# Fusing the weights of keys and queries in 64 by 128 tiles and in two groups, and a first chunk that goes keys, queries, values

## The chip, the cores and the metric

The kernel runs on one core of a Trainium2 chip. The metric is the device time of one execution in microseconds (us). A core has a tensor engine (PE in the profile, with its weight loads shown apart as PEld), a vector engine (DVE), a scalar engine (ACT), a GpSimd engine (POOL) and a queue that issues transfers (SP). Multiplications write to PSUM, which this kernel divides into eight banks of 128 x 512 float32.

## What is computed

The input x has 2048 tokens of 512 numbers. One branch is linear attention with 32 heads of 16 numbers, the other a dense layer with Mish; a sigmoid gate mixes them.

```python
qkv = x @ wqkv                                   # q, k, v: 32 heads of 16
pq, pk = q @ w_phi, k @ w_phi                    # per head, 16 x 16
phi(p) = concat(softmax(p), softmax(-p))         # over the 16, per head: 32 features
kv, z = phi(pk)^T v, sum over tokens of phi(pk)
a = (phi(pq) kv) / (phi(pq) z + 1e-6) @ wo
b = mish(x @ w1 + b1) @ w2
out = g * a + (1 - g) * b,  g = sigmoid((x * gate_w).sum(-1))
```

As pk = (x wk) w_phi = x (wk w_phi), the kernel multiplies the weights first: the 512 x 512 matrix wk with the block-diagonal matrix of w_phi once ("fusing"), and the same for wq. From then on keys and queries are one projection of x each.

## The kernel before

**Two stages.** Stage A runs over 8 chunks of 256 tokens: projections of keys, values and queries, the features of the keys, and the sums over tokens. Stage B runs over 4 blocks of 512 tokens: the dense branch, the features of the queries, the rest of the attention, and the output. The change is all in the first chunk of stage A and in what comes ahead of it.

**Split numbers.** Each float32 operand of a large multiplication is split into a rounded high part and the rest, its low part (names end in h and l): wkh and wkl, xh and xl. A projection of 128 tokens (`proj`, L228) is 12 multiplications of 128 x 512: four 128-row pieces of the depth (k = 0 to 3), times high by high, low by high and high by low. The high part is a copy on ACT (L117), the low part a subtraction on DVE or POOL.

**Fusing.** `fuse` (L214) works for one depth piece k of one matrix. For each of four groups G of eight heads, it multiplies a 128 x 128 block of the transposed weights (as the stationary operand) with a 64 x 64 block of the block-diagonal matrix. L220 does it in four tiles of 64 x 64: two halves r of the rows, each of which has its own PSUM bank, and two halves c of the stationary columns. These operands are plain float32, and the profile shows each such multiplication as two (a load and a multiplication each): 32 loads for one k.

**The order at the start.** SP issues the transfers in the order of the program: wk's first piece, then pieces of x's first chunk and of wk in turn (L147 to L153), both halves of wv (L160), the four pieces of wq (L161), x's second chunk (L163). PE warms up with ten multiplications of ones (L174). The code from L739 on then sets the order on each engine by hand:

- fuse k = 0 and 1 of the keys into four banks (tag "dn"); `fsplit` (L723) splits them, 256 columns at a time, on ACT and DVE; x's first half is split too (`x_one`, L751).
- ten multiplications of the keys' projection (`k_part`, L742, L773), for both 128-token halves in turn; then fuse k = 2 and 3 (L775), two more multiplications, the split of these pieces, and the split of wv: high part on ACT, low part on DVE (L782, L783). The twelve multiplications for k = 2 and 3 end the keys' projection (L784).
- `run(FIRST, ...)` (L810) issues the rest of chunk 0 word by word: v0 and v1 are the values' projections, q0 and q1 the queries'; ve and qe copy them out of PSUM, st stores the queries; mx, mn, d0, d1, E, S, rS, ml are the features of the keys (maximum, minimum, two differences, exponential, sum, reciprocal, product) and z adds them up on POOL; xh and xl split the next chunk's x; ldx and ldw load a later chunk and pieces of w1. The word fq is the fusing of all four pieces of wq in one burst (L790), fh and fl are their splits. So the order on PE is: keys, v0, fusing of wq, v1, q0, q1.

**PSUM.** A pool gives banks in rotation by tag: "a" has three, "dn" four, "kv" one. A bank is written again when its readers are done. Each later chunk goes keys, values, queries by the text MID, with keys and queries in "a" and values in "dn". The sum over tokens (`kv`) takes the bank "kv" from the third chunk on.

Of the kernel before, what the change touches and what calls it, by code (L numbers as in the profile page):

```python
# [19 lines left out]
KT = D // P  # L20
# [15 lines left out]


FIRST = """
    v0 mx0 mn0 d00 d10 mx1 mn1 d01 d11 fq ve0 E0 fh0 fh1 fl0 fl1 fh2 fh3 fl2 fl3 E1 xh xl ldx v1 ve1
    S0 rS0 ml0 z0 ldw0 ldw1 S1 rS1 ml1 z1 q0 qe0 st0 q1 qe1 st1  # L40
"""
MID = """
    k0 xh mx0 mn0 d00 d10 xl ldx k1 wh0 E0 wl0 ldw0 mx1 mn1 d01 d11 v0 wh1 E1 S0 rS0 ml0 z0 ve0 v1 wl1 ldw1
# [42 lines left out]
def tile_gated_mix(ctx: ExitStack, tc: tile.TileContext, xT, wv, wkT, wqT, bd, w1a, w1b, b1, w2a, w2b, wo, out):  # L86
# [6 lines left out]
    pin = tc.keep_in_program_order  # L93
    V, G_, A_, Sy = nc.vector, nc.gpsimd, nc.scalar, nc.sync

    def mm(*a, **k):
        return pin(nc.tensor.matmul(*a, **k))  # L97
# [14 lines left out]
    def psum(name, tag, bufs={"a": 3, "dn": 4, "kv": 1}):  # L112
        nm[0] += 1
        return pp.tile([P, 512], F32, name=f"{name}_{nm[0]}", tag=tag, bufs=bufs[tag])

    def act(out_, in_, fn=AF.Copy, **k):
        return pin(A_.activation(out_, in_, fn, **k))  # L117
# [7 lines left out]
    def f32(ap):  # L125
        return ap.bitcast(F32)
# [8 lines left out]
    skT, sqT = stage(wkT), stage(wqT)  # L135
    bds = k2("bds", "io")[:, :].rearrange("p (g f) -> p g f", g=NG)
# [3 lines left out]
    def ldx(c):  # L140
        rawx[c] = k4("xraw", "tx")
        pin(Sy.dma_start(kt(rawx[c], SC), xT[c]))

    def ldk(dst, src, k):
        pin(Sy.dma_start(dst[:, k, :, :], src[:, k, :, :]))
# [9 lines left out]
    def piece(dram, o, n=1024, small=False):  # L155
        r = k2("raw", "hl") if small else k4("raw", "oh")
        pin(Sy.dma_start(r[:, :n], dram[:, o : o + n]))
        return r[:, :n]

    wvr = [piece(wv, o) for o in (0, 1024)]  # L160
    for k in range(KT):  # L161
        ldk(sqT, wqT, k)
    ldx(1)  # L163


# [30 lines left out]
    def at(key, name, fn):  # L196
        steps.setdefault((key, name), []).append(fn)
# [10 lines left out]
    xs, Es, vs, psA, Ep = {}, {}, {}, {}, {}  # L208
# [5 lines left out]
    def fuse(acc, staged, k):  # L214

        for G in range(NG):
            o = (k % 2 * NG + G) * 64
            for r in (0, 64):
                for c in (0, 64):
                    mm(acc[r // 64][c : c + 64, o : o + 64], staged[r : r + 64, k, G, c : c + 64], bds[r : r + 64, G, r : r + 64], start=True, stop=True, skip_group_check=True)  # L220

    def fuse_banks():
        return [psum("fuse", "dn") for _ in range(2)]

    def halves(w, ks):
        return [w[:, ks, :].rearrange("p k (g r f) -> p r (k g) f", r=2, f=64)[:, r, :, :] for r in range(2)]

    def proj(x, t, wh, wl, tag, lo_last=False):  # L228
        ps = psum("proj", tag)
        xh, xl = x  # L230
        sl = slice(t * P, (t + 1) * P)
        n = 0
        for a, w in ((xh, wh), (xl, wh), (xh, wl)) if lo_last else ((xh, wh), (xh, wl), (xl, wh)):
            for k in range(KT):
                mm(ps, a[k // 2][:, k % 2, sl], w[:, k, :], start=(n == 0), stop=(n == 3 * KT - 1))
                n += 1
        return ps
# [49 lines left out]
    def a_ops(c):  # L287
        key = ("A", c)
        P_ = psA[c] = {}
        for t in range(2):  # L290
            d = {}
            Es[c, t] = d

            def k_(t=t):
                P_["k", t] = proj(xs[c], t, wkh, wkl, "a")

            def v_(t=t):
                P_["v", t] = proj(xs[c], t, wvh, wvl, "dn" if c else ("kv", "a")[t], lo_last=not c)

            def q_(t=t):  # L300
                P_["q", t] = proj(xs[c], t, wqh, wql, "a")

            def ve(t=t):
                if key in THIRD:
                    if t == 0:
                        Ep[key, "v"] = T([P, NFB * 512], F32, "w2b", 2, "v")
                    vs[c, t] = Ep[key, "v"][:, t * 512 : (t + 1) * 512]
                else:
                    vs[c, t] = k2("v", "io")
                act(vs[c, t], P_["v", t])  # L310

            def qe(t=t):
                P_["qs", t] = k2("qs", "pq")
                act(P_["qs", t], P_["q", t])

            def st(t=t):
                i = 2 * c + t
                pin(Sy.dma_start(pqd[i * P : (i + 1) * P, :], P_["qs", t]))

            at(key, f"k{t}", k_)  # L320
            at(key, f"v{t}", v_)
            at(key, f"q{t}", q_)
            at(key, f"ve{t}", ve)
            at(key, f"qe{t}", qe)
            at(key, f"st{t}", st)
            feat_ops(key, t, lambda t=t: P_["k", t][:, :], d)
            at(key, f"ml{t}", lambda d=d: scale_by(d, V))
            at(key, f"z{t}", lambda d=d: pin(G_.tensor_add(zacc, zacc, d["E"])))  # L328

        def kv():  # L330
            if not kvs:
                kvs.append(psum("kvp", "kv")[:, : NG * 64].rearrange("p (g f) -> p g f", g=NG))
            (kvp,) = kvs
            for t in range(2):
                E, v = Es[c, t]["E"], vs[c, t]
                Ev = E[:, :].rearrange("p (a r b x) -> p b r a x", a=2, r=2, b=8)
                for u in range(8):
                    for r in range(2):
                        o = (u % 2) * 64 + 32 * r
                        mm(kvp[o : o + 32, u // 2, :], v[:, u * 64 + 32 * r : u * 64 + 32 * r + 32], Ev[:, u, r, :, :],  # L340
                           start=(c == 0 and t == 0 and u < 2), stop=(c == NCH - 1 and t == 1), skip_group_check=True)

        at(key, "kv", kv)
        if c + 1 < NCH:
            def xh():
                new_x(c + 1)
                for j in range(2):
                    x_hi(c + 1, j)

            at(key, "xh", xh)  # L350
            for j in range(2):
                at(key, "xl", lambda j=j: x_lo(c + 1, j, G_))
        if c + 2 < NCH:
            at(key, "ldx", lambda: ldx(c + 2))
# [368 lines left out]
    def fsplit(acc, k):  # L723
        wh, wl = halves(wkh, slice(k, k + 1)), halves(wkl, slice(k, k + 1))
        src = [a[:, k % 2 * 256 : k % 2 * 256 + 256].rearrange("p (g f) -> p g f", f=64) for a in acc]
        def hi():
            act(wh[0], src[0])
            if k:
                act(wh[1], src[1])
            else:  # L730
                pin(V.tensor_copy(wh[1], src[1]))

        def lo():
            for r in range(2):
                pin(V.tensor_sub(wl[r], src[r], f32(wh[r])))

        return hi, lo

    new_x(0)  # L739
    pk = {}  # L740

    def k_part(k, n):  # L742

        a, w = ((xs[0][0], wkh), (xs[0][1], wkh), (xs[0][0], wkl))[n]
        for t in range(2):
            sl = slice(t * P, (t + 1) * P)
            if t not in pk:
                pk[t] = psum("proj", "a")
            mm(pk[t], a[k // 2][:, k % 2, sl], w[:, k, :], start=(k == 0 and n == 0), stop=(k == KT - 1 and n == 2))

    def x_one(k):  # L751

# [4 lines left out]
    def fused(ks):  # L757
        acc = [fuse_banks() for _ in ks]
        for a, k in zip(acc, ks):
            fuse(a, skT, k)  # L760
        return acc

    acc = fused((0, 1))
# [6 lines left out]
    l1()  # L770
    x_hi(0, 1)
    x_lo(0, 1, V)
    for k, n in ((0, 0), (0, 1), (1, 0), (1, 1), (0, 2)):  # L773
        k_part(k, n)
    acc = fused((2, 3))  # L775
    k_part(1, 2)
    for k in (2, 3):
        for step in fsplit(acc[k - 2], k):
            step()
    for j in range(2):  # L780
        h, l = [w[:, 2 * j : 2 * j + 2, :].rearrange("p k f -> p (k f)") for w in (wvh, wvl)]
        act(h, wvr[j])  # L782
        pin(V.tensor_sub(l, wvr[j], f32(h)))  # L783
    for k in (2, 3):  # L784
        for n in range(3):
            k_part(k, n)

    accq = []

    def fq():  # L790
        for j in range(2):
            accq.extend(fuse_banks())
            for k in (2 * j, 2 * j + 1):
                fuse(accq[-2:], sqT, k)

    at(("A", 0), "fq", fq)
    for i in range(4):
        wh, wl = [halves(w, slice(i // 2 * 2, i // 2 * 2 + 2))[i % 2] for w in (wqh, wql)]

        def ps(i=i):  # L800
            return accq[i][:, :].rearrange("p (g f) -> p g f", f=64)

        at(("A", 0), f"fh{i}", lambda wh=wh, ps=ps: act(wh, ps()))
        at(("A", 0), f"fl{i}", lambda wh=wh, wl=wl, ps=ps: pin(V.tensor_sub(wl, ps(), f32(wh))))

    for t in range(2):
        psA[0]["k", t] = pk[t]
# [69 lines left out]
```

## Time and profile before

| | us |
|---|---|
| median of 3 runs | 445.83 (445.48 to 445.93) |
| profiled execution | 445.67 |
| span of its trace | 443.7 |
| first fusing multiplication | at 5.64 |
| first weight load of chunk 1 | at 26.79 |

The profile is of one execution. A span is the time from the first to the last instruction in the trace; the profiled execution's own time is 1.97 us longer. Rows of the timeline give the start, the length, the engine, the line, the operation with output and inputs, the shape, and how many instructions of a kind follow one another without a gap. Loads of weights (PEld) and multiplications (PE) overlap: the length of a row covers the latency too, and what a row costs PE is read from the start of one to the start of the next. Where idle time stands in brackets, the name behind it is what ended it.

### The profile page before, as it was taken

What the parts mean: (1) busy time and instruction counts of PE and PEld (TensorE: products, weight loads), DVE (VectorE), ACT (ScalarE), POOL (GpSimd) and SP (SyncE); (2) the same over time, 40 slices, a digit from 0 to 9 for tenths busy, and PEclk for the clock granted to TensorE, in tenths of its full rate; (3) what the DMA queues carried; (4) which work ended last, traced back from release to release, by engine and by line L of the source; (5) the groups of instructions that cost most, each with busy time, mean ns of one, the idle gap of its engine ahead of it and who ended that gap; (6) DMA issues with size and microseconds to landing.
All of it is one profiled execution on the core that took longest, in us unless ns stands there. A gap on an engine that the chain in (4) does not pass through costs nothing.

```text
span 443.7 us, 7187 instructions
## 1 busy us (share of the span) xinstructions
PE 439.4 (99%) x2878; PEld 360.8 (81%) x2878; DVE 311.1 (70%) x414; ACT 203.4 (46%) x290; POOL 161.0 (36%) x100
## 2 busy tenths in 40 slices
PE   8999999999999999999999999999999999999997
PEld 7888888888888878887888878888878888887885
DVE  3987839558399999999999898369679329601103
ACT  3644523533435394835466432646352645342331
POOL 3078694785562345541023120215310222411121
PEclk9999999999999999999999999999999999999999
DMA  8721541632404116417353423322605302320002
GB/s 268 279 96 48 191 120 49 188 105 98 158 37 130 49 31 213 125 64 222 120 194 114 146 99 138 94 96 95 191 0 184 102 1 95 122 69 2 0 0 95
DMA packets 28809, 49.11 MB, mean 111 GB/s; under 512 B 6244, under 2 KB 14948, under 8 KB 28776
## 3 DMA queue, kind: packets, MB, share of 16 engines
q1 hardware_dynamic: 28456, 48.26, 33.3%
q8 instruction: 22, 0.36, 0.3%
q10 hardware_dynamic: 288, 0.39, 0.3%
q14 instruction: 11, 0.09, 0.1%
q0 software_dynamic: 32, 0.01, 0.0%
HBM read 31.21 MB, written 16.79 MB: 108 GB/s over the span
## 4 chain that ended last, share of the span: by engine, by line
PE 63%; DVE 3%; ACT 1%; issue 1%
PE down L97 26%; PE up L97 25%; PE wo L97 10%; PE num L97 2%; DVE xbl L429 1%; DVE Sm L274 1%; PE rest L97 0%; DVE E L270 0%; ACT L117 0%; DVE E L285 0%; DVE mn L254 0%; DVE Sm L282 0%; ACT act L117 0%; DVE E L268 0%; ACT h L117 0%
## 5 line engine op out<-in xcount | busy, mean ns | idle before, releaser
L528 POOL TENSOR_TENSOR l<-act,h 128x512 fp32r<-128x512 f32 (+1 forms) x44 | 64.8, 1476 | 214.2 <-ACT h L117 191.8
L117 ACT ACTIVATE act<-up,b1s 128x512 f32<-128x512 f32 x44 | 30.2, 686 | 77.0 <-PE up L97 76.8
L328 POOL TENSOR_TENSOR zacc<-zacc,E 128x1024 f32<-128x1024 f32 x16 | 39.6, 2477 | 40.5 <-DVE E L285 32.0
L117 ACT ACTIVATE E<-E 128x1024 f32<-128x1024 f32 x32 | 33.6, 1061 | 42.1 <-DVE E L270 42.0
L285 DVE TENSOR_TENSOR E<-E,Sm 128x1024 f32<-128x1024 f32 x32 | 47.2, 1475 | 1.0
L97 PE MATMUL wo<-woh,ohl 128*128 128x512 f32 x128 | 41.2, 389 | 0.0
L274 DVE TENSOR_REDUCE Sm<-E 128x64 f32<-128x1024 f32 x32 | 38.6, 1205 | 0.0
L97 PE MATMUL down<-w2ah,h 128*128 128x512 f32 x96 | 37.7, 393 | 0.1
L254 DVE TENSOR_REDUCE mx<-proj 128x32 f32<-128x512 f32 x16 | 11.0, 688 | 30.8 <-PE proj L97 30.8
L97 PE MATMUL down<-w2al,h 128*128 128x512 f32 x80 | 31.2, 390 | 0.0
L97 PE MATMUL down<-w2ah,l 128*128 128x512 f32 x80 | 31.1, 389 | 0.0
L117 ACT ACTIVATE h<-act 128x512 fp32r<-128x512 f32 (+2 forms) x48 | 30.3, 632 | 1.6
L429 DVE TENSOR_TENSOR xbl<-xraw,xbh 128x1024 fp32r<-128x1024 f32 x8 | 12.0, 1528 | 26.8 <-ACT xbh L117 26.8
L97 PE MATMUL down<-w2bh,h 128*128 128x512 f32 x78 | 30.6, 392 | 0.0
L97 PE MATMUL down<-w2bl,h 128*128 128x512 f32 x78 | 30.4, 389 | 0.0
L97 PE MATMUL down<-w2bh,l 128*128 128x512 f32 x78 | 30.4, 389 | 0.0
L97 PEld LDWEIGHTS wo<-woh,ohl 128*128 128x128 f32 x128 | 24.0, 188 | 5.0
L117 ACT ACTIVATE io<-wo,g_sb 128x512 f32<-128x512 f32 x16 | 11.0, 690 | 35.1 <-PE wo L97 32.5
L117 ACT ACT_TABLE_LOAD x19 | 24.4, 1283 | 3.5 <-PE up L97 3.2
L97 PE MATMUL up<-xbh,w1ah 128*128 128x512 f32 x96 | 25.8, 390 | 0.0
L97 PE MATMUL up<-xbh,w1al 128*128 128x512 f32 x96 | 25.7, 389 | 0.0
L97 PE MATMUL up<-xbl,w1ah 128*128 128x512 f32 x96 | 25.7, 389 | 0.0
(126 smaller groups left out, 976.7 us busy)
## 6 DMA issues: line engine op xcount, KB each, us to landing
ed<-E SPq DMA_DIRECT2D x16, 512.0 KB, 2.9
eT<-ed SPq DMA_DIRECT2D x64, 128.0 KB, 3.4
xraw<-in_xT_dram SPq DMA_DIRECT2D x15, 512.0 KB, 5.1
pqd<-qs SPq DMA_DIRECT2D x16, 256.0 KB, 2.2
pq<-pqd SPq DMA_DIRECT2D x16, 256.0 KB, 3.9
out_dram<-io SPq DMA_DIRECT2D x15, 256.0 KB, 2.0
raw<-in_w1a_dram SPq DMA_DIRECT2D x3, 512.0 KB, 6.5
raw<-in_w2a_dram SPq DMA_DIRECT2D x3, 512.0 KB, 4.1
```

Of the source, the lines that this page charges most:

```text
L97: return pin(nc.tensor.matmul(*a, **k))
L117: return pin(A_.activation(out_, in_, fn, **k))
L254: pin(V.tensor_reduce(d[name], hv(src()), axis=AX.X, op=op))
L274: pin(V.tensor_reduce(d["S"], hv(d["E"][:, :]), axis=AX.X, op=ALU.add))
L285: pin(eng.tensor_mul(hv(d["E"][:, :]), hv(d["E"][:, :]), d["S"][:, :, None].to_broadcast([P, 2 * H, DH])))
L328: at(key, f"z{t}", lambda d=d: pin(G_.tensor_add(zacc, zacc, d["E"])))
L429: pin(V.tensor_sub(xb[b][1][:, :, sl], kt(raw[h], SC), f32(xb[b][0][:, :, sl])))
L528: pin(G_.tensor_sub(U[i]["l"][:n, :], U[i]["a"][:n, :], f32(U[i]["h"][:n, :])))
```

## The change

- `fuse` uses tiles of 64 rows by 128 columns: one multiplication in place of the two halves c. The trace of one k has 16 loads in place of 32.
- Pieces k = 2 and 3 of wk and all four of wq are fused in one burst, after twelve multiplications of the keys' projection (before: two bursts, of two pieces after ten, and of four after v0). The six pieces go into three pairs of banks: two of "dn", two of "dn", and one "kv" with one "a". Their splits go 512 columns at a time, high parts on ACT, low parts on DVE, the keys' first.
- The keys' last twelve multiplications come after that burst, with the four that need the low parts of the weights last.
- The low parts of wv are made on POOL in place of DVE, and their high parts come on ACT after the queries' splits.
- `FIRST`: the queries' projections come right after the keys', the values' last. In chunk 0 the values now use banks "a", the queries "dn".
- wv's two transfers are issued after wq's four.

```diff
 FIRST = """
-    v0 mx0 mn0 d00 d10 mx1 mn1 d01 d11 fq ve0 E0 fh0 fh1 fl0 fl1 fh2 fh3 fl2 fl3 E1 xh xl ldx v1 ve1
-    S0 rS0 ml0 z0 ldw0 ldw1 S1 rS1 ml1 z1 q0 qe0 st0 q1 qe1 st1
+    mx0 mn0 d00 d10 q0 E0 qe0 st0 mx1 mn1 d01 d11 xh xl ldx q1 E1 qe1 st1 v0 S0 rS0 ml0 z0 ve0 ldw0 ldw1 v1 S1 rS1 ml1 z1 ve1
 """
...
-    wvr = [piece(wv, o) for o in (0, 1024)]
     for k in range(KT):
         ldk(sqT, wqT, k)
+    wvr = [piece(wv, o) for o in (0, 1024)]
     ldx(1)
...
             for r in (0, 64):
-                for c in (0, 64):
-                    mm(acc[r // 64][c : c + 64, o : o + 64], staged[r : r + 64, k, G, c : c + 64], bds[r : r + 64, G, r : r + 64], start=True, stop=True, skip_group_check=True)
-
-    def fuse_banks():
-        return [psum("fuse", "dn") for _ in range(2)]
+                mm(acc[r // 64][:, o : o + 64], staged[r : r + 64, k, G, :], bds[r : r + 64, G, r : r + 64], start=True, stop=True, skip_group_check=True)
+
+    def fuse_banks(tags=("dn", "dn")):
+        return [psum("fuse", tag) for tag in tags]
...
-                P_["v", t] = proj(xs[c], t, wvh, wvl, "dn" if c else ("kv", "a")[t], lo_last=not c)
+                P_["v", t] = proj(xs[c], t, wvh, wvl, "dn" if c else "a", lo_last=not c)
...
-                P_["q", t] = proj(xs[c], t, wqh, wql, "a")
+                P_["q", t] = proj(xs[c], t, wqh, wql, "a" if c else "dn")
...
-    for k, n in ((0, 0), (0, 1), (1, 0), (1, 1), (0, 2)):
+    for k, n in ((0, 0), (0, 1), (1, 0), (1, 1), (0, 2), (1, 2)):
         k_part(k, n)
-    acc = fused((2, 3))
-    k_part(1, 2)
-    for k in (2, 3):
-        for step in fsplit(acc[k - 2], k):
-            step()
+
+    pairs = (skT, 2, wkh, wkl, ("dn", "dn")), (sqT, 0, wqh, wql, ("dn", "dn")), (sqT, 2, wqh, wql, ("kv", "a"))
+    accs = []
+    for staged, k, _, _, tags in pairs:
+        accs.append(fuse_banks(tags))
+        for i in range(2):
+            fuse(accs[-1], staged, k + i)
+    for (_, k, h, l, _), acc in zip(pairs, accs):
+        wh, wl = halves(h, slice(k, k + 2)), halves(l, slice(k, k + 2))
+        src = [a[:, :].rearrange("p (g f) -> p g f", f=64) for a in acc]
+        for r in range(2):
+            act(wh[r], src[r])
+        for r in range(2):
+            pin(V.tensor_sub(wl[r], src[r], f32(wh[r])))
+    for n in range(3):
+        for k in (2, 3):
+            k_part(k, n, n == 2 and k == 3)
     for j in range(2):
         h, l = [w[:, 2 * j : 2 * j + 2, :].rearrange("p k f -> p (k f)") for w in (wvh, wvl)]
         act(h, wvr[j])
-        pin(V.tensor_sub(l, wvr[j], f32(h)))
-    for k in (2, 3):
-        for n in range(3):
-            k_part(k, n)
+        pin(G_.tensor_sub(l, wvr[j], f32(h)))
...
```

Beyond this, the old words fq, fh and fl and their code (L788 to L804) are gone.

More of the change, by code (lines that the diff above doesn't have):

```diff
@@ L740, in tile_gated_mix, with k_part @@
     pk = {}
-    def k_part(k, n):
+    def k_part(k, n, last=False):
         a, w = ((xs[0][0], wkh), (xs[0][1], wkh), (xs[0][0], wkl))[n]
@@ L748, in k_part @@
                 pk[t] = psum("proj", "a")
-            mm(pk[t], a[k // 2][:, k % 2, sl], w[:, k, :], start=(k == 0 and n == 0), stop=(k == KT - 1 and n == 2))
+            mm(pk[t], a[k // 2][:, k % 2, sl], w[:, k, :], start=(k == 0 and n == 0), stop=last)
     def x_one(k):
@@ L782, in tile_gated_mix @@
         act(h, wvr[j])
-        pin(V.tensor_sub(l, wvr[j], f32(h)))
-    for k in (2, 3):
-        for n in range(3):
-            k_part(k, n)
[L788 to L804, printed above, removed]
+        pin(G_.tensor_sub(l, wvr[j], f32(h)))
     for t in range(2):
```

## The prediction

> **What bounds the kernel now.** I read the page first, then the timeline of the start on PE, then DVE's waits.
>
> ```profile
> span 443.7 us, 7187 instructions
> ...
> PE 439.4 (99%) x2878; PEld 360.8 (81%) x2878; DVE 311.1 (70%) x414; ACT 203.4 (46%) x290; POOL 161.0 (36%) x100
> ...
> PEclk9999999999999999999999999999999999999999
> ```
>
> PE is busy 99% of the span at full granted clock, so what counts is when each multiplication can start. The timeline of the start, and the same stretch in the view by windows (columns: length, then each engine's busy time, clock, DMA share, GB/s):
>
> ```profile
> 5.64 1.39 PE L97 MATMUL fuse<-bds,wT 64*64 64x64 f32 x64
> ...
> 9.48 1.16 PE L97 MATMUL fuse<-bds,wT 64*64 64x64 f32 x64
> ...
> 26.79 0.87 PEld L97 LDWEIGHTS proj<-wkh,xh 128*128 128x128 f32 x4
> ...
> 27.70 0.87 PEld L97 LDWEIGHTS proj<-wkl,xh 128*128 128x128 f32 x4
> ```
> ```profile
> 5.64:27.01 21.37, 21.37 (x329) 17.57 (x329) 19.60 (x33) 11.22 (x21) 3.96 (x3) 1.00 0.68 250
> ```
>
> From the first fusing to chunk 1, PE has work without a hole (21.37 of 21.37). A projection's multiplication costs 0.91/4 = 227 ns, from 26.79 to 27.70. The 72 of chunk 0 are 16.3 us of the stretch; the other 5 are fusing and what surrounds it. Does later work absorb a shift of chunk 1's start? DVE's timeline in chunk 2:
>
> ```profile
> 46.25 0.69 DVE L254 TENSOR_REDUCE mx<-proj 128x32 f32<-128x512 f32 x1 [4.50 <-PE proj L97]
> ```
>
> There DVE waits 4.50 us for PE: the other engines follow PE, and a shift of chunk 1 goes through to the end whole.
>
> **The change: the price of a wider tile.** PE's loads around the burst that fuses wq, and then loads by shape (columns: count | busy us, mean ns of one | idle time):
>
> ```profile
> 15.47 0.87 PEld L97 LDWEIGHTS proj<-wvl,xh 128*128 128x128 f32 x4
> 16.69 1.96 PEld L97 LDWEIGHTS fuse<-bds,wT 64*64 64x64 f32 x128 [0.35 <-issue]
> 18.71 0.76 PEld L97 LDWEIGHTS proj<-wvh,xh 128*128 128x128 f32 x4
> 19.52 0.88 PEld L97 LDWEIGHTS proj<-wvh,xl 128*128 128x128 f32 x4
> ```
> ```profile
> L97 PEld LDWEIGHTS proj<-wvl,xh 128*128 128x128 f32 x64 | 12.0, 188 | 2.5
> ...
> L97 PEld LDWEIGHTS kvp<-E,v 128*32 128x32 f32 x512 | 7.3, 110 | 1.1 <-issue 1.1
> L97 PEld LDWEIGHTS num<-eT,kvb 64*32 64x32 f32 x256 | 4.7, 106 | 2.2 <-issue 0.7 <-DVE Dn L619 0.2
> ...
> L97 PEld LDWEIGHTS fuse<-bds,wT 64*64 64x64 f32 x256 | 4.1, 134 | 1.0 <-issue 0.9
> ...
> L97 PEld LDWEIGHTS down<-w2al,hc 32*128 32x128 f32 x16 | 0.8, 181 | 1.4 <-issue 1.1 <-DMA pq<-pqd 0.4
> ```
>
> The 128 loads start within 1.96 - 0.13 = 1.83 us, one each 14.4 ns, though each lasts 134. Four tiles therefore run side by side, and a **step** of four takes 58 ns. One k has 32 loads, 8 steps; all eight k have 64 steps. After the change a step holds two (the row halves), 16 loads in one k: again 8 steps a k and 64 in all. Half the instructions, the same number of steps: the question is how long a step is.
>
> A load lasts 106 to 110 ns with 32 columns, 134 with 64, 181 to 188 with 128. Rows play no part: 64x32 and 128x32 are alike, 32x128 and 128x128 nearly so. So 64 more columns add 47 to 54 ns to a load, and a step of 128 columns should wait for its load. Two places show how closely 128-column loads can follow:
>
> ```profile
> 209.41 0.19 PEld L97 LDWEIGHTS down<-w2bh,h 128*128 128x128 f32 x1 [0.41 <-ACT ohl L117]
> 209.52 0.19 PEld L97 LDWEIGHTS down<-w2bl,h 128*128 128x128 f32 x1
> 209.75 0.19 PEld L97 LDWEIGHTS down<-w2bh,l 128*128 128x128 f32 x1
> ```
> ```profile
> 439.19 0.19 PEld L97 LDWEIGHTS rest<-w2bh,h 128*128 128x128 f32 x1
> ...
> 440.15 0.19 PEld L97 LDWEIGHTS rest<-w2bh,l 128*128 128x128 f32 x1
> ```
>
> At 209.41, after a pause, with nothing to wait for, the second load starts 110 ns after the first. In the last stretch nine loads, from 439.19 to 440.15, follow each other every 0.96/8 = 120 ns, beside multiplications half as long as a projection's. I take 115 ns for the step (between these two, which are its bounds): 64 x (115 - 58) = **+3.65 us** on PE; by the bounds +3.3 and +4.0.
>
> The Trainium skill, "TensorE: Matmul & The Clock Gate", section "LDWEIGHTS (loading the stationary operand)", says that a load's time goes by its columns, divided by 1.2 to give ns, and not by its rows; 128 columns are 107 ns there. By it the sum would lose 0.5 us of the price: 64 x (107 - 58) = 3.1. The rows above agree with the rule and lie some ns over its figure, so I keep 115.
>
> **What goes away.** (a) One burst: from the load at 15.47 to that at 19.52 are 4.05 us; they hold eight projections (8 x 0.227 = 1.81) and 32 steps (1.86), so entering and leaving a burst costs 0.38. Three bursts become two: **-0.38**. (b) The burst at 5.64 takes 1.39, that at 9.48 with as many multiplications 1.16: the first stands 0.23 for the second piece of wk. With eight steps of 115 the first piece takes 0.45 longer, which covers that: **-0.23**. Sum: 3.65 - 0.38 - 0.23 = **+3.0 us** (by the bounds +2.7 and +3.4).
>
> **What I cost at nothing, and its cover.** The new times on PE by this sum: fusing of k = 0 and 1 from 5.64; the burst of six pieces from about 10.6 (9.48, two multiplications more, 0.45, and 16 x 0.057 - 0.23) to 16.1 (48 x 0.115 = 5.5); keys' last twelve 16.4 to 19.1; queries to 24.6; values to 30.0; chunk 1's first load at 26.79 + 3.0 = 29.8.
>
> ```profile
> 5.41 0.81 SPq L157 DMA_DIRECT2D raw<-in_wv_dram  x2
> ...
> 6.27 1.88 SPq L145 DMA_DIRECT2D wT<-in_wqT_dram  x4
> ```
> ```profile
> DMA to landing us min/median/max: 5.2/6.3/6.6
> ```
> ```profile
> DMA to landing us min/median/max: 4.4/5.9/8.7
> ```
>
> - SP's order. The first landing row is of wv (issues at 5.41 and 5.78, with two later loads by the same line), the second of the pieces of wk and wq. wq now stands where wv stood, a megabyte each: landed by 5.78 + 6.6 = 12.4 at the latest. Its first piece is needed at 10.6 + 16 x 0.115 = 12.4, the last at 15.2. wv, now last, takes wq's place: by about 7.72 + 8.7 = 16.4 (7.72 is the start of the last of the four issues: 6.27 + 1.88 - 0.43). x's second chunk keeps its place. Without this cover PE would stand in the burst, with the keys queued behind.
>
> ```profile
> 11.28 2.03 ACT L117 ACTIVATE wvh<-raw 128x1024 fp32r<-128x1024 f32 x2
> ...
> 12.39 2.36 DVE L783 TENSOR_TENSOR wvl<-raw,wvh 128x1024 fp32r<-128x1024 f32 x2 [0.36 <-ACT wvh L117]
> ...
> 18.24 2.05 ACT L117 ACTIVATE wqh<-fuse 128x512 fp32r<-128x512 f32 x4
> ...
> 19.45 2.47 DVE L804 TENSOR_TENSOR wql<-fuse,wqh 128x512 fp32r<-128x512 f32 x4
> ...
> 40.63 3.38 POOL L383 TENSOR_TENSOR w1al<-raw,w1ah 128x1024 fp32r<-128x1024 f32 x1
> ...
> 43.97 2.41 POOL L328 TENSOR_TENSOR zacc<-zacc,E 128x1024 f32<-128x1024 f32 x1
> ```
>
> - Splits. ACT's six copies of 512 columns take 0.51 each (2.05/4), DVE's subtractions 0.62 (2.47/4). Each pair of pieces takes PE 16 x 0.115 = 1.84, so they keep pace; the last pair's are done 2.5 us after 16.1, at 18.6, ahead of the queries at 19.1, which need its low parts only after four multiplications more.
> - wv's low parts on POOL. ACT has wv's high halves by about 18.6 and 19.6 (1.0 each). POOL needs 2.41 to 3.38 for 128x1024 (rows at 43.97 and 40.63): done at 23.4 to 25.4. The values need them after eight multiplications, at 24.6 + 1.8 = 26.4. Cover 1.0 to 3.0. Behind them on POOL wait the low parts of chunk 1's x, as many elements as one of these (3.38 at most) and needed at 30.0 + 1.8. DVE loses 2.36 us of work.
> - Features of chunk 0: by the rows at 14.67 and 27.21 below they took DVE 14.4 us, 2.47 of it wq's low parts. Without these, from 19.1 on, DVE is free at about 31, and chunk 1's first keys are complete at 30.0 + 2.7 = 32.7. DVE waited 0.84 at that place (row at 29.93).
> - w1's first pieces. Their slots are those of wv's raw halves, so they wait for POOL, and on SP for the queries' stores; issued at about 25 they land 6.5 later, at about 32. ACT wants the first at 31 to 32. Behind it stands an exponential that in the row at 32.45 waited 2.65 for DVE: cover enough.
>
> ```profile
> 7.43 1.41 DVE L735 TENSOR_TENSOR wkl<-fuse,wkh 128x256 fp32r<-128x256 f32 x4
> ...
> 14.67 0.68 DVE L254 TENSOR_REDUCE mx<-proj 128x32 f32<-128x512 f32 x1
> ...
> 27.21 1.88 DVE L285 TENSOR_TENSOR E<-E,Sm 128x1024 f32<-128x1024 f32 x1
> ...
> 29.93 0.69 DVE L254 TENSOR_REDUCE mx<-proj 128x32 f32<-128x512 f32 x1 [0.84 <-PE proj L97]
> ...
> 32.45 1.06 ACT L117 ACTIVATE E<-E 128x1024 f32<-128x1024 f32 x1 [2.65 <-DVE E L270]
> ```
> ```profile
> raw<-in_w1a_dram SPq DMA_DIRECT2D x3, 512.0 KB, 6.5
> ```
>
> - Banks. The burst's banks come free with the splits of k = 0 and 1, done at about 8.84 + 0.7 = 9.5 (row at 7.43); "kv" and the third "a" are unused. The values' banks are those of the keys, free after d1. Nothing late.
>
> Forecast: 445.67 + 3.0 = **448.7 us**, against the profiled execution; the median shown is 0.16 above it.
>
> **Rivals.**
> 1. *Not slower: the load isn't the limit, and a step stays at 58 ns.* For it: the multiplications of a step stay as they are, 64 columns. Against: loads lengthen with columns, and 110 ns is the closest that 128-column loads come. It decides if a step stays below about 67 ns (64 x 9.5 ns = the 0.61 saved). Then only (a) stays, -0.38, as the wait in (b) stays too: 445.3; wq's last piece, wanted at 9.48 + 0.45 + 5 x 0.47 = 12.3, is landed by 12.4.
> 2. *Faster: instructions are the price, and half of them halve the fusing.* 64 steps of 29 ns save 1.86, with (a) 2.2; wq's last piece, wanted at 9.48 + 0.45 + 5 x 0.23 = 11.1 and landed by 12.4, gives back up to 1.3: 443.4 to 444.7, say 444.1. Against: starts every 14.4 ns, loads of 134 ns. The Trainium skill, "TensorEngine Tiling (Array Packing)", "Performance Considerations", gives each matmul an overhead of about 60 cycles, so that very short ones cost the same; this is what would make instructions the price. The row of 128 loads in 1.96 us speaks against it.
> 3. *The two row halves load one after the other.* 64 more loads of 115 ns each: +7.4, 456.1. Against: today four tiles load side by side, two of them in different rows.
> 4. *POOL is late with wv's low parts.* If ACT's copies of wv come over 1 us later than worked out and POOL takes 3.38 each, the values wait on PE with chunk 1 behind; about 1 us more: 449.7.
>
> **How the numbers follow.** Forecast 0.84, rival 1 0.04, rival 2 0.04, rival 3 0.03, rival 4 0.05. The forecast's bounds are 448.3 and 449.1 from the step; 0.4 more on each side stands for the terms read from rows of two decimals and the places of waits. The range, 447.9 to 449.7, takes in rival 4. A difference of 0.2%, 0.9 us, is about what a measurement of this kernel can tell from none: faster 0.04 (rival 2), same 0.04 (rival 1), slower 0.92.
>
> **What the profile after would show.** Fusing in 128 loads, in two rows of 32 and 96, a load lasting about 185 ns, the second row 5.5 us long from about 10.6; no stand in the first; chunk 1's first load at about 29.8; the same distance from there to the end as before. Loads that start every 29 ns (two in 58) make rival 1 right, a row of 96 that ends after 13 us rival 3, and a hole on PE in front of the values' last multiplications rival 4. A hole inside the burst would show wq late. The forecast is wrong if a step is not set by its load, or if chunk 1 catches up.

## The result, and the profile after

| | before | after |
|---|---|---|
| median (us) | 445.88 (445.48 to 447.27, 7 runs) | 449.09 (448.02 to 452.31, 7 runs) |
| ratio, 95% interval | | 1.0075 [1.0055, 1.0096] |
| profiled execution | 445.67 | 448.33 |
| span of its trace | 443.7 | 446.5 |
| first weight load of chunk 1 | 26.79 | 29.57 |

The change makes the kernel slower by 3.2 us in the medians and by 2.66 us between the two profiled executions. The forecast was 448.7, with a range of 447.9 to 449.7. The page of the changed kernel:

```profile
span 446.5 us, 6929 instructions
...
PE 442.1 (99%) x2750; PEld 364.1 (82%) x2750; DVE 308.8 (69%) x410; ACT 203.6 (46%) x288; POOL 166.2 (37%) x102
```

There are 258 instructions fewer, and PE is as full as before: 128 multiplications fewer by the profile's count, each with its load, and yet 2.7 us more of busy time. The timeline of the start, and DVE and ACT further on:

```profile
5.69 2.00 PE L96 MATMUL fuse<-bds,wT 64*128 64x64 f32 x32
...
10.55 5.44 PEld L96 LDWEIGHTS fuse<-bds,wT 64*128 64x128 f32 x96 [0.35 <-issue]
...
16.06 0.76 PEld L96 LDWEIGHTS proj<-wkh,xh 128*128 128x128 f32 x4
...
18.27 4.76 POOL L793 TENSOR_TENSOR wvl<-raw,wvh 128x1024 fp32r<-128x1024 f32 x2 [13.98 <-ACT wvh L116]
...
25.95 0.87 PEld L96 LDWEIGHTS proj<-wvl,xh 128*128 128x128 f32 x4
...
29.57 0.87 PEld L96 LDWEIGHTS proj<-wkh,xh 128*128 128x128 f32 x4
...
32.71 0.69 DVE L252 TENSOR_REDUCE mx<-proj 128x32 f32<-128x512 f32 x1 [1.92 <-PE proj L96]
...
35.23 1.06 ACT L116 ACTIVATE E<-E 128x1024 f32<-128x1024 f32 x1 [2.58 <-DVE E L268]
...
49.03 0.69 DVE L252 TENSOR_REDUCE mx<-proj 128x32 f32<-128x512 f32 x1 [4.50 <-PE proj L96]
```

The second row is the large burst: 96 loads start within 5.44 - 0.19 = 5.25 us (0.19 is the last one's own length). They are 48 steps of two, so a step takes 5.25/47 = 111.7 ns, where four tiles took 58. A load lasts 188 ns, by shape:

```profile
L96 PEld LDWEIGHTS fuse<-bds,wT 64*128 64x128 f32 x128 | 7.3, 188 | 0.6 <-issue 0.4 <-DMA bds<-in_bd_dram 0.2
```

Chunk 1 begins 2.78 us later than before. From there to the end of the span are 416.9 us in both kernels (443.7 - 26.79 and 446.5 - 29.57): in these two executions nothing is caught up, and nothing more is lost. DVE's wait in chunk 2 is 4.50 us as before.

### The profile page after: what moved, and what is told of

Read it like the earlier page. It is cut to its first block, busy times and chain, and to the rows that moved or that the text cites. A ratio compares the mean times of both kernels' runs of the same rounds, so it can differ in the third digit from the quotient of the medians.

```text
span 446.5 us, 6929 instructions
## 1 busy us (share of the span) xinstructions
PE 442.1 (99%) x2750; PEld 364.1 (82%) x2750; DVE 308.8 (69%) x410; ACT 203.6 (46%) x288; POOL 166.2 (37%) x102
## 4 chain that ended last, share of the span: by engine, by line
PE 63%; DVE 3%; ACT 1%; issue 1%
PE down L96 26%; PE up L96 25%; PE wo L96 10%; PE num L96 2%; DVE xbl L427 1%; DVE Sm L272 1%; PE rest L96 0%; DVE E L268 0%; ACT L116 0%; DVE E L283 0%; DVE mn L252 0%; DVE Sm L280 0%; ACT act L116 0%; DVE E L266 0%; ACT h L116 0%
```

## The experiments

All kernels but one are edits of the changed kernel. "Expected" is the text that was on record before the run. Ratios are to the kernel before, which stood at 445.7 to 446.0 beside them.

**The changed kernel again.** No edit.

> The changed kernel once more, unaltered, because its seven runs lie 4.3 us apart (448.02 to 452.31) where those of before lie 1.8 apart. Theory (the price of the change is the longer step of fusing, 111.7 ns in place of 58.3 in the trace, less one burst and one wait): 448.3 to 449.1, with a spread like that of before. Rival (the new order leaves something that is sometimes late): a spread of several us again, while the kernel before, run beside it, stays within 1 to 2 us.

Measured: 448.62 (447.87 to 449.37), ratio 1.006 [1.0045, 1.0076]. The loss is there again, and the runs now lie 1.5 us apart. The profiled execution starts chunk 1 at 30.11, 0.54 later than the one above. The first burst has nearly all of it: 2.50 us in place of 2.00. Timeline, and then two windows within this burst, and the first of these in the execution above:

```profile
5.69 2.50 PE L96 MATMUL fuse<-bds,wT 64*128 64x64 f32 x32
```
```profile
5.70:6.75 1.05, 1.05 (x11) 1.05 (x12) 0.68 (x2) 0.00 (x0) 0.00 (x0) 1.00 1.07 408
6.80:7.90 1.10, 1.10 (x24) 1.10 (x24) 0.53 (x2) 0.38 (x1) 0.00 (x0) 1.00 1.06 391
```
```profile
5.70:6.75 1.05, 1.05 (x21) 1.05 (x20) 0.70 (x2) 0.00 (x0) 0.00 (x0) 1.00 1.07 396
```

With the same operands 11 multiplications (x11) run in the time of 21; in the second window this execution has the full pace too (x24). The clock column says 1.00 throughout, but for the first window it has nothing to go by: the trace's record of the granted clock begins at 6.77 us in this execution and at 5.63 in the one above. Until 6.71 two loads start every 213 ns here, from 6.86 on every 112. The profiled executions of e3, e8 and e9 (below) are as slow until their records begin, at 6.84, 7.01 and 6.28. So PE comes to its full pace at one time or another; that its clock is half until then fits these figures, but no record says it. Up to there the two executions run the same program, so this half microsecond is not the change's doing.

**The wide tile alone**, in the kernel before:

```diff
             for r in (0, 64):
-                for c in (0, 64):
-                    mm(acc[r // 64][c : c + 64, o : o + 64], staged[r : r + 64, k, G, c : c + 64], ...)
+                mm(acc[r // 64][:, o : o + 64], staged[r : r + 64, k, G, :], ...)
```

> The kernel before with the 64x128 tiles alone: three bursts, values ahead of the queries, wv first, wv's low parts on DVE. Theory: 64 steps longer by 53.4 ns are +3.4, less about 0.2 for the wait for wk's second piece: +3.2, about 449.0 against 445.8. Rival (order carries the price): within 0.5 us of the kernel before.

Measured: 448.78 (448.22 to 450.5), ratio 1.0069 [1.0051, 1.0087], +3.1 us. The burst of wq in the timeline:

```profile
18.71 3.65 PEld L97 LDWEIGHTS fuse<-bds,wT 64*128 64x128 f32 x64 [0.35 <-issue]
```

32 steps in 3.65 - 0.19 = 3.46 us, (3.46/31) 111.6 ns each, in another order and another place. The tile's width by itself gives the whole loss. Chunk 1 starts at 30.50 in this execution, whose first burst has the slow start as well (its loads take 2.40 us, in the changed kernel 1.86).

**Multiplications of twice the length.** Is it the load that sets the step, or the multiplication? The moving operand gets 128 columns in place of 64; the results then overwrite each other in the bank, and the kernel no longer computes the fused weights.

```diff
-                mm(acc[r // 64][:, o : o + 64], staged[r : r + 64, k, G, :], bds[r : r + 64, G, r : r + 64], ...)
+                mm(acc[r // 64][:, o % 448 : o % 448 + 128], staged[r : r + 64, k, G, :], bds[r : r + 64, G, :], ...)
```

> The changed kernel with fusing multiplications of 128 moving columns in place of 64 (both blocks of the pair of heads' groups; results overwrite each other in the bank, so the output is not the reference's): same loads, twice the multiplication. Theory (the load of 128 columns sets the step): the step stays near 112, at most 120 ns, so at most +0.5 us against the changed kernel, 448.3 to 449.2. Rival (the multiplication counts in the step beside the load): 112 + 53 = 165 ns, +3.4 us, about 452.

Measured: 448.62 (448.46 to 449.01), ratio 1.006 [1.0045, 1.0075], no longer than the changed kernel. The burst in the timeline:

```profile
10.97 5.63 PE L96 MATMUL fuse<-bds,wT 64*128 64x128 f32 x96
```

5.63 us for multiplications of twice the columns; the changed kernel's take 5.58. They are hidden behind the loads: of the two, the load sets the step.

**The order alone.** The changed kernel with the 64 x 64 tiles of before. If the tile costs 3.4, the order by itself should change little.

```diff
-                mm(acc[r // 64][:, o : o + 64], staged[r : r + 64, k, G, :], ...)
+                for c in (0, 64):
+                    mm(acc[r // 64][c : c + 64, o : o + 64], staged[r : r + 64, k, G, c : c + 64], ...)
```

> The changed kernel with the old tiles of 64x64: the new order, banks, transfers and POOL's share alone. Theory: steps of 58.3 ns again, so the 3.4 us are gone; one burst less saves 0.36; the wait of about 0.2 for wk's second piece is back; and in the burst PE now wants wq's last piece at about 12.3 and gets it at about 13.2, so it stands about 0.9 there. Sum against the kernel before: +0.3 to +0.7, about 446.3, with a hole inside the second burst. Rival (the order, the banks or POOL carry the price, not the tile): 448 or more, with 128x64 loads gone all the same.

Measured: 450.42 (448.22 to 455.71), ratio 1.0097 [1.0072, 1.0123]. The theory fell here: order alone loses 4.7 us, tile alone 3.1, and both together 2.9 to 3.2. The timeline shows a hole in the middle of the large burst (the profiled execution is the slowest of the six):

```profile
10.55 1.94 PEld L96 LDWEIGHTS fuse<-bds,wT 64*64 64x64 f32 x125 [0.35 <-issue]
...
18.12 1.99 PEld L96 LDWEIGHTS fuse<-bds,wT 64*64 64x64 f32 x67 [5.62 <-issue]
```

PE stands 5.62 us, and "issue" means that it waits for nothing that the profile shows; all of wq had landed by 13.3. The windows view (length; PE, PEld, DVE, ACT, POOL busy with counts; clock; DMA share; GB/s), up to the hole and after it:

```profile
0.00:12.42 12.42, 11.14 (x221) 9.97 (x221) 3.90 (x12) 3.82 (x8) 3.37 (x12) 1.00 0.79 252
...
17.30:24.10 6.80, 5.98 (x76) 5.09 (x77) 1.98 (x3) 3.57 (x5) 1.83 (x1) 0.50 0.02 7
```

From 17.30, late in the hole, the granted clock is 0.50 for 6.8 us. And where is the instruction that comes next? The view of the transfers, by queue, for 12.5 to 15.70 and for 15.70 to 15.85:

```profile
q1 hardware_dynamic: 326, 1.16, 99.2%
```
```profile
q1 hardware_dynamic: 9, 0.03, 47.1%
q8 instruction: 1, 0.02, 40.0%
```

A queue of the kind "instruction" moves one packet of 16 KB, which starts at 15.78, and PE goes on 2.3 us later. **New theory: PE runs out of instructions.** It stands where the records run out, not where data is missing. Counted as the profile counts them, 224 multiplications with their loads stand ahead of the hole, 448 records (x221: a few are missing). The kernels that follow test that.

**More instructions ahead.** 65 tiny multiplications of ones ahead of the large burst of the changed kernel, with their 65 x 4 = 260 records:

```diff
+    for i in range(65):
+        c = slice(32 * (i % 4), 32 * (i % 4) + 32)
+        mm(pw[c, :4], ones[c, :32], ones[c, :4], start=True, stop=True, skip_group_check=True)
```

> The changed kernel with 65 tiny multiplications of ones (32 rows, 32 columns, 4 moving; 130 in the trace) ahead of the burst of six pieces. The order alone (64x64 tiles) stood 5.7 us, and the columns in turn 4.1, both after exactly 448 records of PE (loads and multiplications), which is also where wq's third piece begins. Theory of that hole (PE runs out of instructions: the first 448 are there, and the packet with the next ones waits behind the transfers at the start): here the 448th record is 60 into the burst, in the second piece of wk, whose transfer landed long before, and a hole stands there until about 2 us after the first packet of instructions (14.4 to 15.8 in the runs so far), some 3 to 5 us; with the dummies' own 1 to 3 us the time is 452 to 457. Rival (wq's third piece or its banks came late there): no hole in wk's pieces; 449.5 to 452.

Measured: 458.13 (457.59 to 459.35), ratio 1.0276 [1.0255, 1.0298], slightly more than expected: the theory had no price for the clock, which is 0.50 from 16.63 to 26.86. The burst now has a hole that the changed kernel does not have, within the second of its two pieces of wk, whose data had long been there:

```profile
10.89 1.17 PEld L96 LDWEIGHTS warm<-ones 32*32 32x32 f32 x130 [0.35 <-issue]
12.07 1.64 PEld L96 LDWEIGHTS fuse<-bds,wT 64*128 64x128 f32 x28
...
16.84 3.48 PEld L96 LDWEIGHTS fuse<-bds,wT 64*128 64x128 f32 x31 [3.13 <-issue]
```
```profile
0.00:13.58 13.58, 12.46 (x221) 11.37 (x222) 3.86 (x11) 3.16 (x6) 3.37 (x12) 1.00 0.85 276
```

The same count, x221, at another place of the work. The instruction packet comes at 14.52 here, 2.3 us ahead of 16.84; from 12.0 to then queue q1 has the 16 engines full.

**The packet earlier.** In the kernel with small tiles, the loads of wv are issued on ACT's queue after the first pair of splits, so that less bulk stands ahead of the packet.

```diff
-    wvr = [piece(wv, o) for o in (0, 1024)]
+    wvr = []
...
+            if len(wvr) < 2:
+                wvr.append(k4("raw", "oh"))
+                pin(A_.dma_start(wvr[r], wv[:, 1024 * r : 1024 * r + 1024]))
```

> The order alone (64x64 tiles) with wv's two transfers issued by ACT after the first split of the keys' last pieces, at about 12 in place of 7.3: a megabyte less ahead of the packet with PE's instructions. Theory (that packet waits behind the transfers): the hole in the burst shrinks from 4 to 6 us to under 2, and the time is 445.8 to 447.8. Rival (wq's third piece is late by itself, it was ahead of wv anyway): the hole stays at 4 to 6 us, 450 or more.

Measured: 450.18 (449.16 to 451.54), ratio 1.0096 [1.0071, 1.0121]; the time expected was not reached, and it lies in the rival's range, but the hole does not. In the profiled execution the packet came at 12.10 and the hole was 2.50 us:

```profile
14.35 1.99 PEld L96 LDWEIGHTS fuse<-bds,wT 64*64 64x64 f32 x67 [2.50 <-issue]
```

It again ends 2.25 us after the packet, and the clock is 0.5 until 17.7. An earlier packet shortens the hole (two executions compared, of kernels that issue wv at different times); but with 64 x 64 tiles PE comes to its 449th record at 11.9, and a packet at 12.10 is late in any case.

**The records themselves earlier.** The warm-up is 39 tiny multiplications in place of ten large ones (`WARM = 39`, `mm(pw[:32, :32], ones[:, :32], ones[:, :32], ...)`), with small tiles; and the same with wv issued later, as in the last diff.

> The order alone (64x64 tiles) with a warm-up of 39 small multiplications (32 columns, 78 in the trace) in place of ten large ones: 116 records more before the first fusing, in about the same time. Theory (the packet is asked for after a count of records, some 193 by the traces so far, and comes 2 to 5 us later): PE asks at about 6 in place of 10, the packet starts at 9 to 12 and the hole falls to at most 2 us; but the next boundary, 256 records on, then falls at the end of the burst, where a second hole may come. 446 to 450, and a first packet 2 us or more earlier than 15. Rival (the packet's time hangs on the transfers alone): packet at 15 to 16, a hole that starts earlier, in the second or third piece of the burst, and is longer: 452 or more.

> The same warm-up together with wv's transfers issued by ACT at about 12: both remedies for the hole. Theory: the first hole gone or under 1 us, the second shorter than in the run before, as less traffic stands ahead of the second packet; 445.3 to 447.5, the best chance of a version with 64x64 tiles and two bursts that is not slower than the kernel before. Rival: as above, no earlier packet than 12, 449 or more.

Measured: 453.33 (451.73 to 455.03), ratio 1.0169 [1.0145, 1.0193], and 451.95 (449.81 to 453.11), ratio 1.0128 [1.0106, 1.0149]. Neither came near the time expected, but the holes stand where a count puts them. Timelines of the first and of the second:

```profile
11.67 1.95 PEld L96 LDWEIGHTS fuse<-bds,wT 64*64 64x64 f32 x125 [0.56 <-issue]
13.68 0.53 PEld L96 LDWEIGHTS proj<-wkh,xh 128*128 128x128 f32 x3
...
17.59 0.19 PEld L96 LDWEIGHTS proj<-wkh,xh 128*128 128x128 f32 x1 [3.38 <-issue]
```
```profile
9.82 3.22 PEld L96 LDWEIGHTS fuse<-bds,wT 64*64 64x64 f32 x192 [0.35 <-issue]
13.11 0.53 PEld L96 LDWEIGHTS proj<-wkh,xh 128*128 128x128 f32 x3
...
15.50 0.19 PEld L96 LDWEIGHTS proj<-wkh,xh 128*128 128x128 f32 x1 [1.86 <-issue]
```

In the first, the first hole shrinks to 0.56 (its packet came at 8.95, 2.72 us ahead of its end), and a second one comes 128 multiplications later, 256 records, one packet of 16 KB. In the second kernel the first hole is gone, and the second stands at the same instruction. The windows up to this hole:

```profile
0.00:14.24 14.24, 12.60 (x348) 11.20 (x349) 5.94 (x15) 5.69 (x12) 3.37 (x12) 1.00 0.83 281
```
```profile
0.00:13.70 13.70, 12.54 (x349) 11.25 (x349) 5.91 (x15) 5.82 (x11) 3.37 (x12) 1.00 0.80 267
```

224 + 128 = 352 multiplications, x348 and x349 recorded. The packets for these came at 15.23 and 13.07, PE went on 2.36 and 2.43 us later. Behind these holes the clock stays at 1.00. Both kernels stand twice more, at 64 to 68 and at 117 to 121 us; the next kernel shows why.

**Small tiles for three pieces only.** Pieces 1 to 3 of wk in 64 x 64 tiles, the other five wide, so that the 449th record is not in the burst.

```diff
-                mm(acc[r // 64][:, o : o + 64], staged[r : r + 64, k, G, :], ...)
+                for c in (0, 64) if staged is skT and k else (slice(0, P),):
+                    c = slice(c, c + 64) if isinstance(c, int) else c
+                    mm(acc[r // 64][c, o : o + 64], staged[r : r + 64, k, G, c], ...)
```

> The changed kernel with 64x64 tiles for wk's pieces 1, 2 and 3 and 64x128 tiles for the other five. Theory (a wide tile costs 0.43 us a piece, and PE must not come to its 449th record before the first packet of instructions is in, at about 17): 96 records more, so 416 by the end of the burst at about 14.7 and the 449th at about 18.5, no hole from that; 3 x 0.43 less, some 0.2 to 0.4 back where wk's second and wq's last pieces are now waited for: 447.3 to 447.8. Rival (small tiles in this order always bring the hole): 450 or more.

Measured: 450.57 (450.01 to 453.46), ratio 1.011 [1.0086, 1.0133]. The burst has no hole, and chunk 1 starts 0.63 earlier than in the changed kernel, but time is lost further on. The timeline:

```profile
10.62 4.74 PEld L96 LDWEIGHTS fuse<-bds,wT 64*64 64x64 f32 x128 [0.35 <-issue]
...
28.94 0.87 PEld L96 LDWEIGHTS proj<-wkh,xh 128*128 128x128 f32 x4
...
61.90 2.71 PEld L96 LDWEIGHTS kvp<-E,v 128*32 128x32 f32 x189 [0.35 <-issue]
...
65.87 0.14 PEld L96 LDWEIGHTS kvp<-E,v 128*32 128x32 f32 x3 [1.26 <-issue]
```

The sum over tokens, `kvp`, is a burst of 192 short loads; three from its end PE stands 1.26 us, and 1.11 us up to 118.8 once more. The instruction packet came at 63.46, 2.41 us ahead of 65.87. These bursts use records fast, and here the end of a packet falls within them. The changed kernel has exactly 256 records fewer on PE than the one before, a whole packet, so its packets end at the same later instructions as before; this kernel has 160 fewer than before, and they end elsewhere. The two kernels with the small warm-up have 276 records more than this one, 20 more than a whole packet, so there a packet should end ten loads sooner. It does; the first of them:

```profile
63.38 2.60 PEld L96 LDWEIGHTS kvp<-E,v 128*32 128x32 f32 x179 [0.35 <-issue]
67.81 0.26 PEld L96 LDWEIGHTS kvp<-E,v 128*32 128x32 f32 x13 [1.84 <-issue]
```

The second stands after 179 loads too (1.22 us), and in the later burst this kernel stands after 162 loads, those two after 152.

**The same, padded to whole packets.** 40 tiny multiplications of ones after chunk 0 (160 records) bring the count to that of the kernel before.

```diff
+    pd = psum("pad", "dn")
+    for i in range(40):
+        c = slice(32 * (i % 4), 32 * (i % 4) + 32)
+        mm(pd[c, :4], ones[c, :32], ones[c, :4], start=True, stop=True, skip_group_check=True)
```

> The mixed kernel came to chunk 1 at 28.9, 0.6 ahead of the changed kernel, and lost 2.4 us later: in each of the bursts of kvp at 62 and 115 PE stood 1.2 to 1.3 us, and went on 2.4 us after a packet of instructions began. The kernels whose count of PE records differs from that of before by 0, 4 or 256 had no such holes; this one differs by 160. Here 40 tiny multiplications of ones (80 in the trace, 160 records) follow chunk 0, so that the count from there on is that of the kernel before. Theory (the holes come from where the boundaries of 256 records fall): both holes are gone; with 0.7 to 1.1 us for the padding itself the time is 448.6 to 449.4. Rival (they come from something else in the mixed kernel): the holes stay, 451.0 to 451.7.

Measured: 448.80 (448.06 to 449.99), ratio 1.0064 [1.0046, 1.0081]. The timeline, and all waits of PE that the waits view lists:

```profile
63.09 2.73 PEld L96 LDWEIGHTS kvp<-E,v 128*32 128x32 f32 x192 [0.35 <-issue]
```
```profile
PE warm L96 <- DVE ones L166: 1.1, 1, 1.1
PE fuse L96 <- DMA wT<-in_wqT_dram: 0.3, 1, 0.3
```

Both holes in `kvp` are gone, and the kernel with 40 useless multiplications is 1.8 us faster than without. The padding also moves this burst from 61.90 to 63.09, but the burst at 63.38 above has its hole. The count of instructions decided.

**Two that settled less.** *wv first:* the changed kernel with wv's two transfers ahead of wq's, as before.

```diff
+    wvr = [piece(wv, o) for o in (0, 1024)]
     for k in range(KT):
         ldk(sqT, wqT, k)
-    wvr = [piece(wv, o) for o in (0, 1024)]
```

> The changed kernel with wv's transfers ahead of wq's again, as in the kernel before. Theory: wq's four pieces land at about 13.2, 15.2, 15.9 and 16.5 as they did before, the burst wants them at 12.4, 13.3, 14.2 and 15.1, so PE stands about 0.8 for the first and 1.1 for the second: +1.9 us against the changed kernel, about 450.5. Rival (transfers are hidden either way): 448.3 to 449.1.

Measured: 451.08 in the median of four (449.46, 454.81, 449.73, 452.43), ratio 1.0142 [1.0089, 1.0196]. That is near the theory's 450.5, but the two stands of 0.8 and 1.1 us are not shown: the profiled execution is the fastest of the four, has one stand of 0.27 us in the burst, and comes to the burst 0.64 us late for the slow start that the changed kernel's second execution shows. The two slower runs have a mean granted clock of 0.988 and 0.992 (the others 1.00 and 0.999), so part of each ran at a lower clock; what they waited for was not seen. *Columns in turn:* the changed kernel with 64 x 64 tiles and the loop over c outermost, so that only tiles of one column half follow each other.

```diff
-        for G in range(NG):
-            o = (k % 2 * NG + G) * 64
-            for r in (0, 64):
-                mm(acc[r // 64][:, o : o + 64], staged[r : r + 64, k, G, :], ...)
+        for c in (0, 64):
+            for G in range(NG):
+                o = (k % 2 * NG + G) * 64
+                for r in (0, 64):
+                    mm(acc[r // 64][c : c + 64, o : o + 64], staged[r : r + 64, k, G, c : c + 64], ...)
```

> The changed kernel with 64x64 tiles, but all of one column half ahead of the other, so that only two tiles (the row halves) can run side by side: twice the instructions of the changed kernel, each load half as wide. Theory (a step is as long as its load, whatever runs beside it): steps of 58.3 ns, 16 of them for a k, 0.933 us in place of 0.894: +0.3 us against the changed kernel, 448.6 to 449.3, a hole for wq not seen. Rival (a step with two tiles in it takes 112 ns, because only two run side by side): 16 x 0.112 = 1.79 us for a k, +7 us, about 456. Second rival (the PE reorders and finds four tiles again): about as the order alone, 446.3.

Measured: 451.54 (451.37 to 452.58), ratio 1.0131 [1.0112, 1.0149]: the burst meets the hole at x221, 4.03 us. Until then it runs so:

```profile
10.81 2.54 PEld L96 LDWEIGHTS fuse<-bds,wT 64*64 64x64 f32 x125 [0.35 <-issue]
```

(2.54 - 0.13)/124 = 19.4 ns a load, so 39 ns for two of 64 columns, where two of 128 take 112. None of the three expected that. Twice the columns cost nearly three times as much; why was not settled.

## Why the prediction was right, and where it was not

**The step of fusing: right, a little too long.** It takes 111.7 ns, not 115. By the measured step the term is 64 x (111.7 - 58) = 3.44 in place of 3.65. That the multiplication's length does not set it is shown by e5, that the tile alone gives the loss by e3. The load's columns alone are not the whole account: two loads of 64 columns in e4 take 39 ns, well under half of 112. Rivals 1, 2 and 3 (58, 29 and 2 x 115 ns) are out by that one row.

**The small terms.** With -0.38 and -0.23, and 0.04 because the first fusing starts later for the transfer of bds, the sum is 2.87; chunk 1 is 2.78 later. In the wide first burst no stand is left, as said. The -0.38 shows between e3, which has three bursts, and the changed kernel, which has two: 30.50, less 0.54 for the slow start, is 29.96, and the changed kernel is at 29.57, 0.39 sooner (one execution of each). From its bounds the lower end of the forecast is 448.4, not 448.3.

**What was costed at nothing.** The burst ran from 10.55 to 16.0 (10.6 to 16.1), without a hole; wq's last piece landed at about 13.2, later than the 12.4 worked out, but was wanted at 15.0. POOL had wv's low parts at 23.0, wanted at 25.95: rival 4 is out. DVE waited 1.92 us at chunk 1's first maximum (1.7 worked out); ACT's cover was 2.58 (2.65). The distance from chunk 1 to the end is the same.

**Where the working had a gap, and luck.** The sum has no term for the supply of instructions. In the changed kernel none was needed, but the prediction gives no reason for that, so that part is luck. With the 64 x 64 tiles of before, this order brings PE to its 449th record within the burst, at about 12.4, while the packet for it came at 15.78 (e2). In the kernel before that record falls at about 17, behind a packet at 12.98; in the changed kernel at about 30, behind a packet at 14.4, since the wide tiles halve the fusing's instructions. So the worth of tile and order can't be added up: the order alone loses 4.7 us, where the sum of its small terms would have it save some tenths. The wide tile's steps cost 3.4 us in both orders, and in this order it saves a hole (5.62 us in e2's profiled execution, 4.03 in e4's) and the half clock behind it. Rivals 1 and 2 have the wide tile too, so this hole is no objection to them; the measured step is. Nothing in the profile before shows a price of an instruction packet; the queue of the kind "instruction" stands in its list, though, and the count to the 449th record could have been made. That the forecast lies 0.4 us from both the profiled execution and the median is luck in part as well: a slow start moves chunk 1 by 0.5, and the two executions compared both had their clock record begin ahead of the first fusing (at 5.53 and 5.63).

The Trainium skill, "Runtime: NRT & Kernel Launch", section "Instruction fetch mechanics", says that an engine's instructions are refilled in blocks of 16 KiB, 256 of them, by a queue that the sequencer drives itself, and that crossing a block is mostly hidden. The runs agree on the block (stops 256 records apart, packets of 16 KB), and the kernels before and after agree on the rest: 22 and 21 such packets, and no hole. They do not agree on "mostly hidden" where PE runs short instructions: holes of 0.56 to 5.62 us at the start, and 1.26 us in e9 at 65 us, where the transfer engines were busy for about half of the time (share 0.53 from 62.0 to 65.8). What tells the two groups apart is whether the end of a packet falls within a burst of short instructions.

**What stays open.** What the slowest runs waited for (452.31 of the changed kernel, 454.81 of e8): no profile holds one. Why two loads of 64 columns take 39 ns and two of 128 take 112. When a packet is asked for, and why the half clock follows some holes and not others. No version here beat the kernel before; e9 without its later holes, and without the padding that took them away, would be nearest by its start of chunk 1, 28.94 against 26.79.

## What to carry to other kernels

Here a step of small multiplications was as long as its loads allowed, not as its multiplications: four tiles of 64 columns side by side took half the time of two of 128 (58 and 112 ns), though they are twice the instructions. But count the instructions too: bursts of many short ones can outrun their supply. Holes on PE put down to "issue", with a packet on an instruction queue some 2.3 us ahead of their end, were that here; and an edit that shifts the count by less than a packet opened and closed such holes far from itself.

## What the runs showed of the hardware

- PE stopped after 448 records in e2, e4, e6, e7 and e10, and after 704 in e10 and e11, whatever stood there, and went on 2.25 to 2.72 us after the start of a 16 KB packet on the instruction queue.
- At the start this packet comes sooner with less bulk ahead of it: at 15.78 in e2 and 12.10 with wv issued later (e7), at 15.23 in e10 and 13.07 in e11. That it waits behind the bulk transfers is argued from these pairs; full engines alone do not hold it up, for in the kernel before it came at 12.98 while queue q1 filled 98.6% from 11.5 to 17.
- A hole of some microseconds can have an aftermath: the granted clock was 0.50 for 6.8 us from the hole of e2, 3.4 from those of e4 and e7, 10.2 from that of e6. Behind the hole of 3.38 us in e10 it was 1.00.
- In the first microsecond of fusing, PE may run at half pace (11 multiplications in place of 21) until the trace's record of the clock begins. The clock column shows 1.00 for a window that has no record.
